# A first normalisation in two halves, and a table that places every step of the weight units

## The chip, the cores and the metric

The kernel runs on one core of a Trainium2 chip. Its engines are called PE (TensorE, matmuls), DVE (VectorE), ACT (ScalarE), POOL (GpSimd) and SP (SyncE, which here only issues DMAs); each works through its own queue in order. The metric is the device time of one execution in microseconds (us), the median of several runs.

## What is computed

```python
def _attn_ref(q, k, v, g_norm):          # q, k, v: (8, 8, 576, 64)
    kv = np.einsum('bhsd,bhse->bhde', k, v)
    out = np.einsum('bhsd,bhde->bhse', q, kv)
    rms = np.sqrt(np.mean(out * out, axis=-1, keepdims=True) + 1e-06)
    return (out / rms * g_norm).astype(np.float32)

def _moe_ref(x, w_in, w_out, a, b):      # x: (4608, 512), w_in: (512, 2048), w_out: (2048, 512)
    h = x @ w_in
    h2 = h * h
    h3 = h2 * h
    P = a[0] + a[1] * h + a[2] * h2 + a[3] * h3
    Q = 1.0 + np.abs(b[0]) * np.abs(h) + np.abs(b[1]) * h2
    g = P / (Q + 1e-06)
    return (g @ w_out).astype(np.float32)
```

x is the attention's output, all eight heads of a token side by side. The weights come as 64 bit floats.

## The kernel before

The 4608 tokens are nine tiles (t) of 512. A tile has 16 slots (c), one for each 128 columns of w_in and 128 rows of w_out. The main loop (L598) counts slots i = 16 t + c through all tiles. In a slot PE does gemm2 of two slots before (LAG = 2, four accumulators in PSUM), steps of the next tile's attention, and gemm1 of the next slot into one of two PSUM buffers h. ACT, DVE and POOL turn h into g in four steps: ew_a (ACT v and u, DVE q and u, L417 to L420), ew_b (ACT q, Ln, Exp into a PSUM bank r, DVE u, L426 to L429), ew_c (DVE u, r, g, L435 to L442) and, one slot later, ew_d (ACT gh, POOL gl, L452 and L453). A buffer h is free once L427 has read it.

A 32 bit product at full precision is made of parts: a factor is cast to fp32r (the high part) and the difference is kept as a second part; a gemm is then three matmuls, high by high, low by high and high by low. In tile 0 the first four gemm1 and the first twelve gemm2 take whole 32 bit factors instead (unsplit1, unsplit2; PE makes two passes of each).

A weight unit, such as ("wi", 4), is two slots' weights, 1024 columns of 64 bit words. It is fetched to a raw tile (fetch_w, L166) and converted on the chip: "hi" and "lo" scale its high and low words (scale_high and scale_low, L180 on ACT or L182 on DVE), "shift" (L203) and "or" (L208) on DVE and "add" (L209, on POOL as a rule) put a 32 bit float together in ups, and split_w casts it (L224, ACT) and subtracts (L225, POOL). The tables scale_at, conv_at and split_at (L143 to L152) give each unit a slot for each stage; fetch_at gives the slot of its fetch. These steps fill tile 0's slots; the splits of the first six wo units lie in tile 1. L209 on DVE shows in the trace as a custom operation.

Ahead of the loop stands the attention of tile 0: the loads `first` (k, v, q and constants of each of four head pairs p), first_kv (kvp, L540; copies kvf, L543), first_o (op, L547; square sq, L549; xf, L550), the means ms (L570), the reciprocal root in three ACT and two DVE steps (newton_rstd, L250 to L256), its spread over the partitions by a matmul (rb, L588) and the norm (L589). warm (L531) issues matmuls on a zero tile whose result nobody reads. For later tiles the same runs in steps inside the slots (att_kv, att_o, att_ms, att_rstd, att_rd, att_rb, att_norm), the spread as a DMA to DRAM and back; split makes the two parts of x (ACT L264, then L268), for tile 1 in slot 14.

All this stands in a manual schedule: the order of the code is the order of each engine's queue.

## Time and profile before

| what | us |
|---|---|
| median of 3 runs (910.95 to 911.41) | 911.12 |
| the profiled execution | 911.83 |
| its span, first to last instruction | 910.0 |
| PE busy in the span | 886.8 |
| ACT / DVE / POOL busy | 710.5 / 694.0 / 342.8 |

A line of the timeline gives start, duration, engine, line of the code, operation, the tiles written and read, shape and count, and in brackets how long the engine stood idle before it and who released it. A line of the waits gives who waited for whom, the sum, the count and the longest. In a group of instructions stand the busy time and the mean duration of one in ns. Durations of neighbours overlap a little, since the engines are pipelined.

### The profile page before, as it was taken

What the parts mean: (1) busy time and instruction counts of PE and PEld (TensorE: products, weight loads), DVE (VectorE), ACT (ScalarE), POOL (GpSimd) and SP (SyncE); (2) the same over time, 40 slices, a digit from 0 to 9 for tenths busy, and PEclk for the clock granted to TensorE, in tenths of its full rate; (3) what the DMA queues carried; (4) which work ended last, traced back from release to release, by engine and by line L of the source; (5) the groups of instructions that cost most, each with busy time, mean ns of one, the idle gap of its engine ahead of it and who ended that gap; (6) DMA issues with size and microseconds to landing.
All of it is one profiled execution on the core that took longest, in us unless ns stands there. A gap on an engine that the chain in (4) does not pass through costs nothing.

```text
span 910.0 us, 12075 instructions
## 1 busy us (share of the span) xinstructions
PE 886.8 (97%) x4372; PEld 693.9 (76%) x4372; DVE 694.0 (76%) x1029; ACT 710.5 (78%) x1171; POOL 342.8 (38%) x272
## 2 busy tenths in 40 slices
PE   9799979999999999999999999999999999999997
PEld 6355547778888788878887888788878887887886
DVE  2999997677876777677777777678667877787776
...
GB/s 368 233 239 117 127 68 42 116 53 48 11 118 82 48 1 128 81 21 27 116 57 36 48 84 85 41 48 41 120 20 47 1 70 12 48 1 47 1 1 46
DMA packets 24485, 65.94 MB, mean 72 GB/s; under 512 B 2345, under 2 KB 3369, under 8 KB 24425
## 3 DMA queue, kind: packets, MB, share of 16 engines
q1 hardware_dynamic: 23848, 64.65, 21.9%
...
q10 hardware_dynamic: 576, 0.52, 0.2%
...
## 4 chain that ended last, share of the span: by engine, by line
PE 80%; DVE 11%; ACT 5%; issue 3%; ACTq 0%; POOL 0%; DVEq 0%; POOLq 0%
PE h L407 13%; PE acc L472 12%; PE h L409 12%; PE h L408 12%; PE acc L474 12%; PE acc L473 12%; PE kvp L297 2%; DVE q L419 2%; DVE u L435 1%; DVE r L436 1%; PE idle L531 1%; ACT r L428 1%; ACT q L426 1%; DVE u L427 1%; PE op L328 1%
## 5 line engine op out<-in xcount | busy, mean ns | idle before, releaser
L453 POOL TENSOR_TENSOR gl<-u,gh 128x512 fp32r<-128x512 f32 x131 | 172.5, 1317 | 453.3 <-ACT gh L452 266.6
L407 PE MATMUL h<-x,wiparts 128*128 128x512 f32 (+1 forms) x564 | 226.4, 401 | 0.0
L409 PE MATMUL h<-x,wiparts 128*128 128x512 f32 (+1 forms) x564 | 219.6, 389 | 1.1 <-DVE x L268 1.1
L408 PE MATMUL h<-x,wiparts 128*128 128x512 f32 (+1 forms) x564 | 219.2, 389 | 0.0
L435 DVE SCALAR_TENSOR_TENSOR u<-u,na,r 128x512 f32<-128x512 f32 x143 | 106.7, 746 | 88.9 <-ACT r L429 88.8
L419 DVE SCALAR_TENSOR_TENSOR q<-v,b0abs,h 128x512 f32<-128x512 f32 x143 | 106.2, 743 | 83.2 <-ACT u L418 83.0
L417 ACT ACTIVATE v<-h,b 128x512 f32<-128x512 f32 x143 | 98.8, 691 | 90.1 <-PE h L409 86.6
L407 PEld LDWEIGHTS h<-x,wiparts 128*128 128x128 f32 x564 | 105.9, 188 | 30.2 <-DVE u L427 5.9
L426 ACT ACTIVATE q<-q 128x512 f32<-128x512 f32 x143 | 90.6, 634 | 48.2 <-DVE q L419 47.2
L409 PEld LDWEIGHTS h<-x,wiparts 128*128 128x128 f32 x564 | 105.9, 188 | 24.8 <-DVE x L268 2.3
L474 PE MATMUL acc<-woh,gl 128*128 128x512 f32 x320 | 124.6, 389 | 0.0
L473 PE MATMUL acc<-wol,gh 128*128 128x512 f32 x320 | 124.5, 389 | 0.0
L472 PE MATMUL acc<-woh,gh 128*128 128x512 f32 x320 | 124.5, 389 | 0.0
L408 PEld LDWEIGHTS h<-x,wiparts 128*128 128x128 f32 x564 | 106.1, 188 | 21.4 <-issue 1.3
L418 ACT ACTIVATE u<-h,na 128x512 f32<-128x512 f32 x143 | 111.2, 778 | 0.0
L427 DVE SCALAR_TENSOR_TENSOR u<-u,na,h 128x512 f32<-128x512 f32 x143 | 106.8, 747 | 4.6
L428 ACT ACTIVATE r<-q,bias 128x512 f32<-128x512 f32 x143 | 99.0, 692 | 4.6
L452 ACT CAST gh<-u 128x512 fp32r<-128x512 f32 x131 | 81.5, 622 | 23.9 <-DVE u L442 23.2
L429 ACT ACTIVATE r<-r,bias 128x512 f32<-128x512 f32 (+1 forms) x145 | 95.6, 659 | 4.8
L436 DVE SCALAR_TENSOR_TENSOR r<-q,r 128x512 f32<-128x512 f32 x143 | 98.3, 687 | 0.0
L420 DVE TENSOR_TENSOR u<-u,h 128x512 f32<-128x512 f32 x143 | 97.1, 679 | 0.0
L442 DVE SCALAR_TENSOR_TENSOR u<-r,u 128x512 f32<-128x512 f32 x131 | 90.4, 690 | 4.1
...
## 6 DMA issues: line engine op xcount, KB each, us to landing
...
```

The costliest lines, as they stand in the source:

```text
L407: PE.matmul(ph, wh, xh, start=(kc == 0), stop=False)
L408: PE.matmul(ph, wl, xh, start=False, stop=False)
L409: PE.matmul(ph, wh, xl, start=False, stop=(kc == NPAIR - 1))
L418: ACT.activation(u, ph, AF.Identity, bias=na[:, 2:3], scale=na[:, 3:4])
L419: DVE.scalar_tensor_tensor(q, v, b0abs, ph, ALU.add, ALU.mult)
L427: DVE.scalar_tensor_tensor(u, u, na[:, 1:2], ph, ALU.add, ALU.mult)
L428: ACT.activation(r, q, AF.Ln, bias=bias[:, 2:3], scale=QSC)
L435: DVE.scalar_tensor_tensor(u, u, na[:, 0:1], r, ALU.add, ALU.mult)
L453: POOL.tensor_tensor(gl, u, f32(gh), ALU.subtract)
L472: PE.matmul(o, gh[:, ss], wh, start=(c == 0), stop=False)
L473: PE.matmul(o, gh[:, ss], wl, start=False, stop=False)
L474: PE.matmul(o, gl[:, ss], wh, start=False, stop=(c == NF - 1))
```

## The change

The first normalisation is done in two halves of two head pairs each: ms, the three ACT and two DVE steps, rb and the norms of pairs 0 and 1 are issued between the products of pairs 2 and 3, and gemm1 of slot 0 in two halves too. The loads of `first` come pair by pair, with the small copy into `spread` after pair 0's. Most of the matmuls of warm are gone. Pair 3's xf is made on ACT.

scale_at, conv_at and split_at give way to a table, first_tiles. Each entry names a step, its engine (A, D or P for ACT, DVE or POOL), and a slot with a place in it: s before ew_a, h between the ACT and DVE halves of ew_a, q before ew_b, v inside ew_b ahead of Ln, e behind ew_b, r at the start of ew_c, g ahead of the DVE step that makes g, z at the end. Units x0 and x1 are the x of tiles 0 and 1 by head pair. Fetches move to other slots, one raw tile to another room, and the reciprocal root of tile 1 one slot later. Of the longer removed blocks, all in the listing above, the diff shows nothing ("...").

```diff
-        ("wi", 6): "p6", ("wo", 2): "r0", ("wi", 8): "p5", ("wo", 4): "r1",
+        ("wi", 6): "p6", ("wo", 2): "p4", ("wi", 8): "p5", ("wo", 4): "r1",
...
-        -1: [("wi", 6), ("wo", 2)], 0: [("wi", 8), ("wo", 4)], 2: [("wi", 10), ("wo", 6)], 4: [("wi", 12), ("wo", 8)],
-        6: [("wi", 14)], 8: [("wo", 10)], 10: [("wo", 12)], 11: [("wo", 14)],
+        -1: [("wo", 2), ("wi", 6)],
+        1: [("wi", 8), ("wi", 10), ("wo", 6)],
+        2: [("wo", 4)],
+        4: [("wi", 14)],
+        5: [("wo", 8)],
+        6: [("wi", 12)],
+        7: [("wo", 10)],
+        9: [("wo", 12)],
+        10: [("wo", 14)],
     }
...
+    first_tiles = {
+        ("wi", 4): "hi A 0s, lo A 0z, shift D 0g, or D 1h, add P 1v, cast A 2h, rest P 2q",
+        ("wi", 6): "hi A 1z, lo A 1h, shift D 2s, or D 2r, add P 3e, cast A 4q, rest P 4z",
+        ("wi", 8): "hi A 3e, lo A 4e, shift D 4v, or D 4z, add P 5e, cast D 6q, rest P 7v",
+        ("wi", 10): "hi A 5h, lo A 6z, shift D 6g, or D 7h, add P 7v, cast A 7v, rest P 8s",
+        ("wi", 12): "hi A 7q, lo A 8q, shift D 8v, or D 8r, add P 8r, cast A 9g, rest P 10e",
+        ("wi", 14): "hi A 10q, lo A 10q, shift D 10v, or D 11s, add P 11h, cast A 12q, rest P 12e",
+        ("wi", 0): "cast D 7v, rest P 7r",
+        ("wi", 2): "shift2 D 0s, or2 D 0s, add2 P 0q, cast A 3s, rest P 3v",
+        ("wo", 0): "shift D 0s, or D 0s, add P 0s, cast A 15g, rest P 16z",
+        ("wo", 2): "hi D 0z, lo A 2q, shift D 1r, or D 1z, add P 2v, cast D 17z, rest D 19r",
+        ("wo", 4): "hi A 3e, lo A 3r, shift D 3z, or D 4h, add P 4v, cast A 18z, rest P 21e",
+        ("wo", 6): "hi A 5v, lo D 5r, shift D 5r, or D 5r, add P 6v, cast A 21v, rest P 23s",
+        ("wo", 8): "hi A 6z, lo A 7z, shift D 7e, or D 7z, add P 9g, cast A 24s, rest D 24v",
+        ("wo", 10): "hi A 9q, lo D 10s, shift D 9r, or D 9g, add P 10q, cast D 24z, rest P 25q",
+        ("wo", 12): "hi A 10r, lo A 12h, shift D 11r, or D 12h, add D 12h, cast A 12r, rest D 13e",
+        ("wo", 14): "hi A 11g, lo A 13r, shift D 12g, or D 13s, add P 14s, cast A 14g, rest D 14z",
+        ("x0", 0): "cast A 0s, rest D 0s",
+        ("x1", 0): "norm P 13h, cast A 14e, rest D 14g",
+        ("x0", 1): "cast A 0h, rest P 1v",
+        ("x1", 1): "norm P 11g, cast D 14r, rest P 14z",
+        ("x0", 2): "cast A 0h, rest D 0v",
+        ("x1", 2): "norm D 14e, cast A 14r, rest P 15s",
+        ("x0", 3): "cast A 1s, rest P 2z",
+        ("x1", 3): "norm P 13v, cast A 14r, rest P 15h",
+    }
+    plan = {}
+    for u, row in first_tiles.items():
+        for entry in row.split(", "):
+            what, by, at = entry.split()
+            plan.setdefault((int(at[:-1]), at[-1]), []).append((what, {"A": ACT, "D": DVE, "P": POOL}[by], u))
+
+    def todo(i, place):
+        for what, by, u in plan.pop((i, place), ()):
+            steps[what](by, u)
...
-    def conv_b2(u, part=both, add_by=POOL):
+    def conv_or(u, part=both):
-        add_by.tensor_tensor(w, w, low, ALU.add)
+    def conv_add(u, part=both, by=POOL):
+        low, high = words(u, part)
+        w = ups[u].bitcast(I32)[:, part]
+        by.tensor_tensor(w, w, low, ALU.add)
...
+    def copy(by, to, of):
+        ACT.copy(to, of) if by == ACT else by.tensor_copy(to, of)
...
-        for js in (one, two) if c == SPLIT0 else (both,):
-            ACT.copy(wh[:, js], w[:, js])
-            POOL.tensor_tensor(wl[:, js], w[:, js], f32(wh[:, js]), ALU.subtract)
+        wparts[u] = wh, wl
+        copy(by, wh, ups[u])
+    def rest_w(u, by):
+        wh, wl = wparts.pop(u)
+        by.tensor_tensor(wl, ups.pop(u), f32(wh), ALU.subtract)
...
-    for f, at in ((att_kv, [1, 3, 5, 7]), (att_o, [2, 4, 6, 8]), (att_ms, [9]), (att_rstd, [9]), (att_rd, [10]), (att_rb, [11, 11]), (att_norm, [12, 12, 13, 13])):
+    for f, at in ((att_kv, [1, 3, 5, 7]), (att_o, [2, 4, 6, 8]), (att_ms, [10]), (att_rstd, [10]), (att_rd, [11]), (att_rb, [11, 12])):
...
         ACT.activation(u, ph, AF.Identity, bias=na[:, 2:3], scale=na[:, 3:4])
+        between()
         DVE.scalar_tensor_tensor(q, v, b0abs, ph, ALU.add, ALU.mult)
         DVE.tensor_tensor(u, u, ph, ALU.mult)
...
-        fill(-1)
         ACT.activation(q, q, AF.Abs)
         DVE.scalar_tensor_tensor(u, u, na[:, 1:2], ph, ALU.add, ALU.mult)
+        between()
         ACT.activation(r, q, AF.Ln, bias=bias[:, 2:3], scale=QSC)
...
     for p in range(NPAIR):
-        nc.sync.dma_start(kvq0[p][:, 0:10 * P], first[p][:, 0:10 * P])
-    for p in range(NPAIR):
-        nc.sync.dma_start(kvq0[p][:, 10 * P:], first[p][:, 10 * P:])
+        for part in (slice(0, 10 * P), slice(10 * P, NC0 + 8)):
+            nc.sync.dma_start(kvq0[p][:, part], first[p][:, part])
+        if p == 0:
+            nc.sync.dma_start(quarters[:, 1, D:P], quarters[:, 0, 0:D])
     fetch_w(("wi", 0))
-    nc.sync.dma_start(quarters[:, 1, D:P], quarters[:, 0, 0:D])
...
+        if p == 3:
+            ACT.activation(xf[0, p], o0[p], AF.Copy, scale=ghalf)
+        else:
+            DVE.tensor_scalar(xf[0, p], o0[p], ghalf, None, ALU.mult)
...
     warm(8, idle)
-    for p in range(NPAIR):
-        first_kv(p)
-        warm(3, idle)
+    r0 = work.tile([P, TW], F32, tag="u", name="r_0")
+    r2 = work.tile([P, TW], F32, tag="u", name="r2_0")
+    ms0 = {}
+
+    def first_ms(k):
+        pool, tag = ((ps_at, "at"), (ps_at, "r"))[k]
+        ms0[k] = pool.tile([P, TW], F32, tag=tag, name=f"ms_0_{k}", bufs=1)
+        for p in (2 * k, 2 * k + 1):
+            PE.matmul(ms0[k][p * Q4:(p + 1) * Q4], sel, sq0[p], start=True, stop=True)
+
+    def first_newton(k):
+        ps = slice(2 * k * Q4, 2 * (k + 1) * Q4)
+        ms, r, rr = ms0[k][ps], r0[ps], r2[ps]
+        return (
+            lambda: ACT.activation(r, ms, AF.Ln, bias=bias[ps, 0:1], scale=ZSC),
+            lambda: ACT.activation(r, r, AF.Exp, bias=bias[ps, 1:2], scale=-0.5),
+            lambda: ACT.activation(rr, r, AF.Square),
+            lambda: DVE.scalar_tensor_tensor(rr, ms, 1e-6, rr, ALU.add, ALU.mult),
+            lambda: DVE.scalar_tensor_tensor(r, rr, 3.0, r, ALU.subtract, ALU.mult),
+        )
+
+    rb0 = {}
+
+    def first_rb(p):
+        rb0[p] = ps_acc.tile([P, TW], F32, tag="acc", name=f"rb_0_{p}")
+        ps = slice(p * Q4, (p + 1) * Q4)
+        PE.matmul(rb0[p], spread[ps], r0[ps], start=True, stop=True)
+
+    def first_norm(p):
+        DVE.tensor_tensor(xf[0, p], xf[0, p], rb0[p], ALU.mult)
+
+    first_kv(0)
+    warm(3, idle)
     POOL.tensor_scalar(ghalf, gcol, -0.5, None, ALU.mult)
     POOL.tensor_scalar(na, ab[:, 0:4], -1.0, None, ALU.mult)
     POOL.tensor_copy(b1, ab[:, 5:6])
-    for p in range(NPAIR):
-        first_o(p)
+    first_o(0)
+    first_kv(1)
+    first_o(1)
+    first_kv(2)
+    first_ms(0)
+    newton = first_newton(0)
+    newton[0]()
+    first_o(2)
+    first_kv(3)
+    for step in newton[1:3]:
+        step()
+    conv_a(("wi", 0), one, DVE)
+    conv_b1(("wi", 0), one)
+    for step in newton[3:]:
+        step()
+    conv_b2(("wi", 0), one)
+    first_o(3)
+    first_ms(1)
+    first_rb(0)
+    first_rb(1)
+    newton = first_newton(1)
+    for step in newton[:3]:
+        step()
     fetch_kvq(1, 0)
     for u in fetch_at[-1]:
         fetch_w(u)
...
+    first_norm(0)
+    conv_a(("wi", 0), two)
+    first_norm(1)
+    for step in newton[3:]:
+        step()
+    h00 = ps_h.tile([P, TW], F32, tag="h", name="h_0_0")
+    gemm1_part(0, 0, h00, slice(0, TW), (0, 1))
+    first_rb(2)
+    first_rb(3)
     ACT.activation(b0abs, ab[:, 4:5], AF.Abs)
+    conv_b1(("wi", 0), two)
+    conv_b2(("wi", 0), two)
+    first_norm(2)
+    first_norm(3)
+    gemm1_part(0, 0, h00, slice(0, TW), (2, 3))
     for part in (one, two):
         conv_a(("wi", 2), part)
...
     conv_b1(("wi", 2), one)
     conv_b2(("wi", 2), one)
     conv_a(("wo", 0))
...
+    steps = {
+        "hi": lambda by, u: scale_high(u, by),
+        "lo": lambda by, u: scale_low(u, by),
+        "shift": lambda by, u: conv_b1(u),
+        "or": lambda by, u: conv_or(u),
+        "add": lambda by, u: conv_add(u, both, by),
+        "shift2": lambda by, u: conv_b1(u, two),
+        "or2": lambda by, u: conv_or(u, two),
+        "add2": lambda by, u: conv_add(u, two, by),
+        "cast": lambda by, u: cast_w(u, by) if u[0] in ("wi", "wo") else xl1.update({u: split(int(u[0][1]), u[1], by)}),
+        "rest": lambda by, u: rest_w(u, by) if u[0] in ("wi", "wo") else xl1.pop(u)(by),
+        "norm": lambda by, u: by.tensor_tensor(xf[1, u[1]], xf[1, u[1]], rbs[1, u[1] // 2][u[1] % 2], ALU.mult),
+    }
     for i, (t, c) in enumerate(slots[:-1]):
-        ew_a(t, c, ph)
+        rest = {0: [], 1: [], 2: []}
+        todo(i, "s")
+        ew_a(t, c, ph, between=lambda: todo(i, "h"))
         if i:
             ew_d(*slots[i - 1])
...
+        todo(i, "q")
+        ew_b(t, c, ph, r_bank(t, c), lambda: todo(i, "v"))
+        todo(i, "e")
         if i >= LAG:
             gemm2(*slots[i - LAG])
...
-        if 4 <= i < len(slots) - 2 and not early:
+        if 4 <= i < len(slots) - 2:
             ph = gemm1(*slots[i + 1])
-        if c == NF - 2 and t < NTILE - 1:
+        if c == NF - 2 and 0 < t < NTILE - 1:
             xl = [split(t + 1, p) for p in range(NPAIR)]
             for k in range(2):
                 rest[k].append(xl[k])
                 rest[2].append(xl[2 + k])
-        ew_c(t, c, lambda k: [f() for f in rest[k]])
-        if i in scale_at and scale_at[i][0] == "wi":
-            scale_low(scale_at[i], ACT)
-        if i >= NF and i in split_at:
-            split_w(split_at[i])
+        ew_c(t, c, lambda k: [todo(i, "rgz"[k]), *(f() for f in rest[k])])
     finish(NTILE - 1)
```

More of the change, by code (lines that the diff above doesn't have):

```diff
@@ L257, in newton_rstd, with split @@
         return rest
-    def split(t, p, low_by=DVE):
+    def split(t, p, by=ACT):
         if p % 2 == 0:
@@ L263, in split, with rest @@
         f = xf[t, p]
-        ACT.copy(xh, f)
+        copy(by, xh, f)
         x.setdefault(t, []).append((xh, xl))
-        def rest():
+        def rest(low_by=DVE):
             low_by.tensor_tensor(xl, f, f32(xh), ALU.subtract)
@@ L397, in gemm1, with gemm1_part @@
         return ph
-    def gemm1_part(t, c, ph, cs):
-        for kc in range(NPAIR):
+    def gemm1_part(t, c, ph, cs, kcs=range(NPAIR)):
+        for kc in kcs:
             ks = slice(kc * P, (kc + 1) * P)
@@ L409, in gemm1_part, with ew_a @@
             PE.matmul(ph, wh, xl, start=False, stop=(kc == NPAIR - 1))
-    def ew_a(t, c, ph, w=TW):
+    def ew_a(t, c, ph, w=TW, between=lambda: None):
         nm = f"{t}_{c}"
```

67 lines of the change are left out of this document (9 added, 58 removed).

## The prediction

> **What bounds the kernel now.** I read the busy time by stage first, then PE's own waits, then the rows around each wait. Columns of the stage table: window and length in us, busy us (and count) of PE, PEld, DVE, ACT, POOL, granted clock, DMA share, GB/s.
>
> ```profile
> 22.00:50.00 28.00, 22.33 (x74) 9.95 (x71) 27.67 (x34) 19.50 (x32) 18.68 (x12) 1.00 0.58 212
> 50.00:110.00 60.00, 59.08 (x248) 34.62 (x247) 59.41 (x71) 52.83 (x83) 36.82 (x21) 1.00 0.45 157
> 110.00:144.00 34.00, 26.43 (x90) 17.60 (x88) 31.70 (x37) 23.38 (x35) 24.05 (x12) 0.90 0.28 82
> 144.00:165.00 21.00, 19.20 (x115) 14.56 (x115) 15.46 (x26) 17.76 (x31) 7.86 (x5) 1.00 0.28 90
> 165.00:265.00 100.00, 100.00 (x515) 81.22 (x515) 75.36 (x119) 85.02 (x141) 46.02 (x31) 1.00 0.22 66
> ```
>
> From 165 us on PE is never idle: the change touches nothing there that PE waits for, so the end moves by what PE gains before 165. There PE idles 28.00 - 22.33 = 5.67, 0.92, 7.57 and 1.80 us, 15.96 in all, while DVE is full until 144. The waits of PE between 22 and 170 us give the same sum and the culprits:
>
> ```profile
> PE acc L468 <- DVE g L442: 6.0, 2, 3.7
> PE acc L472 <- ACT woparts L224: 3.6, 1, 3.6
> PE acc L473 <- POOL woparts L225: 1.7, 1, 1.7
> PE h L403 <- POOL wiw L209: 1.2, 1, 1.2
> PE h L409 <- DVE x L268: 1.1, 2, 0.9
> PE acc L472 <- ACT ob L480: 0.6, 1, 0.6
> ```
>
> Why DVE is full shows where it works beside POOL, and in the groups of 50 to 110 us (busy, then mean ns of one):
>
> ```profile
> 47.17 2.37 POOL L225 TENSOR_TENSOR wiparts<-wiw,wiparts 128x1024 fp32r<-128x1024 f32 x1 [0.55 <-ACT wiparts L224]
> 47.90 2.73 DVE L208 SCALAR_TENSOR_TENSOR wow<-raw_wo,wow 128x1024 int32<-128x1024 int32 x1
> L208 DVE SCALAR_TENSOR_TENSOR wiw<-raw_wi,wiw 128x1024 int32<-128x1024 int32 x4 | 4.8, 1212 | 0.0
> L182 DVE TENSOR_SCALAR raw_wi<-raw_wi 128x1024 f32<-128x1024 f32 x4 | 7.6, 1891 | 0.0
> L180 ACT ACTIVATE raw_wi<-raw_wi 128x1024 int32<-128x1024 uint32 x5 | 5.8, 1167 | 0.0
> L224 ACT CAST wiparts<-wiw 128x1024 fp32r<-128x1024 f32 x5 | 5.3, 1056 | 2.0 <-POOL wiw L209 2.0
> ```
>
> The same L208 costs 1.21 us with POOL quiet and 2.73 when POOL is at work: POOL ends at 47.17 + 2.37 = 49.54, and DVE ends 1.09 later, so it stood still until then. The Trainium skill says so too ("SBUF — State Buffer", section "SBUF: two separate sides"): the port pair of DVE and GpSimd is held for a whole instruction and the other engine blocks. The trace agrees, with these 1.09 us. By that rule every copy and difference that this change gives to DVE also shuts POOL out, which speaks against the change; it is the first rival below.
>
> **Term A, the start up to the first gemm2.** Before, one chain runs through all four pairs:
>
> ```profile
> 10.41 0.80 PE L540 MATMUL kvp<-first 128*64 128x64 f32 x20
> 11.26 0.42 ACT L543 COPY kvf<-kvp 64x64 f32<-64x64 f32 x2 [1.17 <-PE kvp L540]
> 11.92 3.60 PE L547 MATMUL op<-first,kvf 128*128 128x512 f32 x8
> 15.45 1.80 PE L570 MATMUL ms<-sq,sel 128*32 128x512 f32 x8
> 17.35 0.69 ACT L250 ACTIVATE r<-ms,bias 128x512 f32<-128x512 f32 x1 [1.20 <-PE ms L570]
> 19.55 0.69 DVE L255 SCALAR_TENSOR_TENSOR r<-ms,r 128x512 f32<-128x512 f32 x1 [0.88 <-ACT r L252]
> 19.51 2.34 ACT L180 ACTIVATE raw_wi<-raw_wi 128x512 f32<-128x512 f32 x4
> 21.07 1.25 PE L588 MATMUL rb<-r,spread 32*128 32x512 f32 x8 [0.49 <-issue]
> 22.20 2.48 DVE L589 TENSOR_TENSOR xf<-xf,rb 128x512 f32<-128x512 f32 x4 [1.23 <-PE rb L588]
> 26.49 1.39 POOL L209 TENSOR_TENSOR wiw<-wiw,raw_wi 128x512 int32<-128x512 int32 x1 [6.45 <-DVE wiw L208]
> 27.94 7.13 PE L403 MATMUL h<-xf,wiw 128*128 128x512 f32 x16 [1.24 <-POOL wiw L209]
> 30.35 0.73 DVE L427 SCALAR_TENSOR_TENSOR u<-u,na,h 128x512 f32<-128x512 f32 x1
> 32.57 1.49 DVE L203 TENSOR_SCALAR wiw<-raw_wi 128x512 int32<-128x512 int32 x1
> 34.09 2.77 DVE L208 SCALAR_TENSOR_TENSOR wiw<-raw_wi,wiw 128x512 int32<-128x512 int32 x1
> 38.70 0.68 DVE L442 SCALAR_TENSOR_TENSOR g<-r,u 128x512 f32<-128x512 f32 x1
> 39.52 3.67 PE L468 MATMUL acc<-wow,g 128*128 128x512 f32 x8 [3.72 <-DVE g L442]
> 10.00:12.00 2.00, 2.00 (x32) 1.81 (x31) 0.00 (x0) 0.51 (x3) 0.55 (x3) 1.00 1.06 411
> ```
>
> The eight loads of the first tile are 4 x (640 + 260) KB, 9 us at 411 GB/s, full from about 3 us: all in at 12. After the change they come pair by pair, and SP holds pair 1 behind the copy of L525 until POOL has filled its source, so I put pair 3 at 12.5. Its chain: kvp (0.80 as at 10.41) to 13.6 after a wait for op of pair 2, the two kvf copies (0.42) to 14.1, op (a quarter of 3.60) to 15.05. On ACT the first half's Exp and Square stand ahead of its square, so that ends at 16.05; ms 17.0; Ln to Square (17.35 to 19.55 before, 2.2) 19.2; two L255/L256 steps 20.8; rb (1.13 to its reader) 21.9; norms 23.2, against 22.20 + 2.48 = 24.68 before. The first half (rb at 17.05, norms to 19.4) lets h(0,0) run two of its four passes beside this; the other two end at 24.3. The second half of the first weight unit, added at 26.49 + 1.39 = 27.88 before, gets its scaling on ACT at 19.2, two DVE steps by 21.65, POOL's 1.3: 23.0. So h(0,1) starts at 24.3 instead of 27.94.
>
> Little of these 3.6 us counts yet. h(0,2) takes the buffer that slot 0's L427 frees. On ACT, from 19.2, wi0's two half scalings (1.2), wi2's four (2.34 as at 19.51), wo0's two and wi4's one (1.17 each by L180) and an x cast stand ahead of v, 7.3 in all: v at 26.5. On DVE, five steps of wi2, wo0 and x0 come first: q at 28.5, L427 30.4 as before. PE idles 2.8 us; h(0,2) runs 30.5 to 33.95, kvp to 34.7. What is gained lies behind L427: L203 and L208 of 32.57 and 34.09 (4.2 us) are already done. L435 goes at 31.65 when Exp has ended, then L436, one shift, L442: g ends at 34.15 instead of 39.38, and gemm2(0,0) starts at 34.7 instead of 39.52. **A = 4.8.** Bounds: one more POOL operation of 2.4 in DVE's way leaves 2.4; if L427 waits for nothing, h(0,1), h(0,2) and kvp run through to 31.9, and 7.6 is gained.
>
> **Term B, slots 2 to 10.** PE has only 0.92 us to give. The high scaling of six wi units goes from DVE (1.89 each) to ACT (1.17 each by L180): 7.6 us leave a DVE that is full, and ACT, at 52.83 of 60, takes 4 x 1.17 = 4.7 and gives wi8's and wi0's casts (1.06 each) to DVE and a low scaling of wo6: about 54.3 of 60. Summed by slot from these rows, elementwise work included, DVE has 4.4 to 7.1 us per slot in slots 2 to 11, ACT 4.3 to 8.5 (the 8 and 8.5 in slots 3 and 10, each followed by a lighter one), PE 7.0. PE ends last in the sums; POOL's waits take half a microsecond, most likely before h(0,4), whose last x difference is POOL's third job in slot 2. **B = 0.5** (0 to 0.9; 3.0 if the long first pass of each gemm1 goes too, 0.79 in the row below against 0.40, seven times 0.3).
>
> ```profile
> 50.47 0.79 PE L407 MATMUL h<-x,wiparts 128*128 128x512 f32 x1
> ```
>
> **Term C, slots 11 to 14.** Here the waits of 2.3, 3.6 and 1.7 us lie, and a half clock behind them:
>
> ```profile
> 124.97 2.21 DVE L209 CUSTOM_DVE_ANT_0 wow<-raw_wo,wow 128x2048 uint16<-128x2048 uint16 x1
> 36.00:38.00 2.00, 0.00 (x0) 0.00 (x0) 2.00 (x3) 0.00 (x0) 1.37 (x2) 1.00 0.00 0
> 133.00:134.00 1.00, 1.00 (x3) 0.81 (x4) 0.97 (x2) 1.00 (x2) 1.00 (x1) 0.50 0.00 0
> ```
>
> wo12 and wo14 are converted on DVE inside slots 12 and 13, with such an add of 2.2 us in each, g comes late, ACT's cast of wo12 stands behind gh, POOL's difference behind that. At half clock some 3.5 us are worked, so 1.8 are lost: C is at most 7.57 + 1.8 = 9.4. After, the scalings are on ACT in 10 and 11, wo14's add is on POOL, both differences are on DVE. Counted from the start of gemm2(0,10): PE wants wo12's difference after gemm2, h, gemm2, h (3.43 + 2.74 each) at 12.4. DVE in slots 12 and 13 has: POOL's norm to wait for (1.5), or 1.1, add 2.2, elementwise 3.8, wo14's shift and or 1.7, half a slot of elementwise 1.9, POOL's next norm 1.5, difference 1.1: 14.8. So 2.4 us of waiting stay, and no gap is long. **C = 9.4 - 2.4 = 7.0**; with both old waits for the parts still there, 2.3.
>
> **Term D, slots 14 to 17.** The x differences of tile 1 are spread over slots 14 and 15; POOL's last one ends 1.5 us before PE reads it by my count, so 1.1 goes and the evacuation's 0.6 stays. **D = 1.1** (0 to 1.8). POOL is handed two norms, three x differences and wo14's add there, 10 us in three slots of 5.5 to 6.2: it fits, but the last link has 1.5 us of cover.
>
> Other moves cost nothing on PE: the wo casts and differences of slots 16 to 25 have the ACT (85.02) and POOL (46.02) of the last stage row as cover, and each stands one slot or more ahead of its gemm2.
>
> **Sum:** 4.8 + 0.5 + 7.0 + 1.1 = 13.4. The profiled execution took 911.83 (span 910.0); less 13.4 it is 898.4. The median of the runs shown is 0.7 lower, so I predict 897.7.
>
> **Rivals.**
> 1. The port. Each difference or cast new on DVE meets POOL's 2.4 us jobs and waits about 2.73 - 1.21 = 1.5; then DVE keeps its pace: A half, B nothing, C near its low end: 2.4 + 2.8 = 5.2, 906. For it: DVE's 59.41 of 60. Against: per two slots one port step goes from DVE to ACT, which has a port of its own. Chance 0.14.
> 2. The clock. The change drops 23 of 34 warm-up calls, and PE waits in pieces between 9 and 24 us. Run at half clock from 12 to 24, the two last op passes (0.9 each), ms and rb (1 each) and h(0,0) (3.4) cost 7 more: gain 6.4, 905. Against: 3.7 idle us at 35.8 left 1.00 (row of 36 to 38). The Trainium skill ("TensorE: Matmul & The Clock Gate", section "What's actually happening") halves the clock after an idle window of about 3.4 us; by that rule the start, with no gap over 1.5 in my chain up to h(0,1), stays at full clock; the gap at 35.8, 3.9 long, might have lost it by the same rule and did not. I give it 0.06.
> 3. Slower: the loads. Weight fetches now stand on SP behind steps that wait: wo6 behind wi4's add, wi12 behind a qr whose buffer op frees, wo12 and wo14 behind POOL adds one slot ahead of their use. ACT then waits for data in front of its elementwise work.
>
> ```profile
> 90.32 0.38 SPq L166 DMA_DIRECT2D raw_wo<-in_w_out_dram  x1
> 97.17 1.19 ACT L180 ACTIVATE raw_wo<-raw_wo 128x1024 f32<-128x1024 f32 x1 [0.47 <-DMA raw_wo<-in_w_out_dram]
> ```
>
> A load took 6.9 us from issue to use here (97.17 - 90.32); wi12 has some 4, one gemm1 and the first two ACT steps of a slot. From 3.4 us each at four places that reach PE (13.4 / 4) it is slower; at 5 each, 20 - 13.4 = 6.6 slower: 918. For it: ACT waited in the row of 97.17 already. Against: h has two buffers and gemm2 lags two slots, so a wait under some 3 us is covered. Chance 0.12.
> 4. The waits move and the sum is nothing, 911: 0.03.
>
> **Chances and range.** The forecast has 0.65, from 889 to 903: its own bounds are A 7.6, B 3.0, C 9.4, D 1.8, sum 21.8, 889, and, with two terms at their low ends, 8 us, 903. Up to 907 come rivals 1 and 2. Range 889 to 907, about 0.8. The measurement tells 0.2% (1.8 us) from no change: faster 0.85, same 0.03, slower 0.12.
>
> **What would show it.** A: PE's first L468 group at about 35 instead of 39.5, h(0,1) near 24, L427 of slot 0 near 30. B: L182 on DVE gone for wi, DVE below 56 of 60 in slots 3 to 10. C: no half clock, one wait of about 2 us on wo12's difference. D: no wait of gemm1(1,0) on x. Wrong if the page shows ACT waiting on weight DMAs for more than 3 us at a time, L208 still near 2.7 in most slots, or idle PE behind 165.

## The result, and the profile after

The changed kernel takes 903.12 us (median of 4 runs, 901.94 to 903.68); the kernel before took 911.26 beside it (910.95 to 912.42). The ratio is 0.9907 (95% interval 0.9889 to 0.9924): 8 us faster, where 13.4 were forecast. The profiled execution is the slowest of the four, 903.68, with a span of 901.9 (before 910.0).

The lines of the code have moved. What the prediction calls L403 is now L442 (whole gemm1), L407 to L409 are L446 to L448 (gemm1 in parts), L468 is L508 (whole gemm2), L472 to L474 are L512 to L514 (gemm2 in parts), L180 and L182 are L209 and L211 (scalings), L203, L208 and L209 are L232, L237 and L242 (shift, or, add), L224 is L249 (casts), L225 is L266 (weight differences), L268 is L307 (x differences), L427 is L466 (frees h) and L442, the step that writes g, is L482.

Busy time by stage of the changed kernel, columns as in the prediction:

```profile
22.00:50.00 28.00, 24.19 (x83) 11.44 (x79) 26.82 (x38) 25.62 (x39) 18.05 (x11) 1.00 0.80 300
50.00:110.00 60.00, 56.67 (x240) 33.35 (x239) 55.28 (x72) 51.82 (x80) 40.32 (x22) 1.00 0.42 152
110.00:144.00 34.00, 30.49 (x110) 21.30 (x109) 29.27 (x38) 25.20 (x37) 19.75 (x12) 0.90 0.14 32
144.00:165.00 21.00, 21.00 (x130) 17.30 (x129) 15.87 (x27) 19.53 (x35) 9.53 (x7) 1.00 0.41 138
165.00:265.00 100.00, 99.97 (x516) 81.06 (x514) 77.74 (x121) 82.12 (x138) 39.34 (x29) 1.00 0.19 59
128.00:130.00 2.00, 2.00 (x6) 1.56 (x5) 1.97 (x4) 1.53 (x4) 2.00 (x1) 0.50 0.00 0
```

DVE is no longer full behind 50 us, as forecast (55.28 of 60). PE now idles 3.81 us from 22 to 50 (before 5.67), 3.33 from 50 to 110 (before 0.92), 3.51 from 110 to 144 (before 7.57), none to 165. So the second stage has become worse, and the third, at a mean clock of 0.90 again, still holds a half clock, of which the last row shows a part. The longest waits of PE from 18 to 175 us:

```profile
PE acc L513 <- DVE woparts L266: 3.4, 1, 3.4
PE h L442 <- POOL wow L242: 3.0, 1, 3.0
PE acc L508 <- POOL wow L242: 2.7, 1, 2.7
PE h L442 <- DVE xf L629: 1.6, 2, 0.9
PE h L448 <- POOL x L307: 0.4, 1, 0.4
```

None of before's long waits is left in its old form; three take their place, each about 3 us long. Two the prediction had (3.0 ahead of h(0,2), where it counted 2.8; 3.4 on wo12's difference, where it counted 2.4). The 2.7, a gemm2 that waits for an add on POOL, it had not.

To see where the time came from I compare the start of the same work in the traces: of the first matmul of gemm2(0,n), the gemm2 with w_out rows 128 n of tile 0, which stands in slot n + 2 (n = 16 and 23 run on into tile 1). Each entry is before's start less that kernel's start, in us, so a gain up to there. The experiments' columns are used further down. The last row gives the times at which the granted clock of that trace falls to 0.50 (up to 900 us). Each such stretch lasts 3.41 us, those with a star 6.83 us, and a busy PE loses half of it. Where it falls differs between traces whose code is the same up to there, so a part of every column is chance.

| n | start before | changed | s_start | t_table | e1 | e3 | e5 | e7 | e6 | e9 | e11 |
|---|---|---|---|---|---|---|---|---|---|---|---|
| 0 | 39.52 | 3.2 | 1.0 | -1.0 | 2.4 | 1.8 | 2.4 | 1.6 | 1.4 | 1.7 | 2.7 |
| 7 | 92.05 | 3.9 | -0.5 | 0.8 | 3.2 | 3.5 | 4.0 | 3.3 | 3.1 | 3.4 | 3.4 |
| 9 | 105.58 | 0.9 | -0.5 | -3.2 | 2.5 | 3.5 | -2.0 | 3.3 | -0.9 | 3.4 | 2.7 |
| 13 | 139.98 | 4.5 | -0.3 | 4.9 | 4.0 | 8.8 | 6.7 | 9.9 | 6.4 | 8.4 | 9.1 |
| 14 | 147.26 | 6.4 | -0.4 | 6.8 | 5.9 | 7.3 | 8.5 | 8.1 | 8.3 | 9.4 | 8.7 |
| 16 | 161.11 | 7.4 | -0.4 | 7.4 | 6.9 | 8.0 | 9.1 | 5.7 | 9.3 | 10.0 | 9.2 |
| half clock from | 129.71* | 126.44* | 37.64*, 129.80* | 35.81, 100.66 | 126.82* | 31.90, 134.30 | 31.49, 96.34* | 32.23, 141.46 | 32.43, 97.28 | 32.63, 124.79 | none |

In the terms of the prediction: A 3.2 (forecast 4.8); from there to n = 7, most of B, 0.7 (0.5); then 3.0 are lost again by n = 9; from 9 to 14, C, 5.4 (7.0); from 14 to 16, D, 1.0 (1.1). At n = 23 (206 us) the gain is 7.1, at the end of the span 8.1: the last 1.0 comes behind 206 us, 0.4 of it up to PE's last matmul (905.32 and 897.86), 0.6 behind that, while the last output is written.

**Start of the changed kernel.** Its timeline (start, duration, engine, line):

```profile
19.65 1.96 PE L442 MATMUL h<-xf,wiw 128*128 128x512 f32 x4 [0.87 <-DVE xf L629]
23.51 5.42 PE L442 MATMUL h<-xf,wiw 128*128 128x512 f32 x12 [0.78 <-DVE xf L629]
25.32 1.36 POOL L242 TENSOR_TENSOR wiw<-wiw,raw_wi 128x512 int32<-128x512 int32 x1 [1.15 <-DVE wiw L237]
25.56 1.68 DVE L237 SCALAR_TENSOR_TENSOR wiw<-raw_wi,wiw 128x512 int32<-128x512 int32 x1
29.62 0.74 DVE L459 SCALAR_TENSOR_TENSOR q<-v,b0abs,h 128x512 f32<-128x512 f32 x1
31.07 0.75 DVE L466 SCALAR_TENSOR_TENSOR u<-u,na,h 128x512 f32<-128x512 f32 x1
31.96 3.67 PE L442 MATMUL h<-xf,wiw 128*128 128x512 f32 x8 [3.04 <-POOL wow L242]
34.34 0.68 DVE L482 SCALAR_TENSOR_TENSOR g<-r,u 128x512 f32<-128x512 f32 x1
36.30 1.12 PE L508 MATMUL acc<-wow,g 128*128 128x512 f32 x2
```

The chain has the forecast's shape. h(0,0) begins with two of its four head pairs at 19.65, the rest follow at 23.51; q comes at 29.62 (forecast 28.5), L466 starts at 31.07 (forecast, as L427, 30.4), h(0,2) at 31.96 (30.5), g ends at 35.02 (34.15), and the first gemm2 starts at 36.30 (34.7). About one microsecond is lost ahead of q: the "or" at 25.56 lies beside POOL's add of 25.32 and takes 1.68, where the same shape took 0.69 without one.

**Around 90 us.** POOL, DVE and the gemm2 that waits:

```profile
84.81 2.41 POOL L266 TENSOR_TENSOR wiparts<-wiw,wiparts 128x1024 fp32r<-128x1024 f32 x1
85.03 3.26 DVE L237 SCALAR_TENSOR_TENSOR wow<-raw_wo,wow 128x1024 int32<-128x1024 int32 x1
92.33 2.44 POOL L242 TENSOR_TENSOR wiw<-wiw,raw_wi 128x1024 int32<-128x1024 int32 x1 [5.11 <-ACT xf L372]
94.72 2.38 POOL L242 TENSOR_TENSOR wow<-wow,raw_wo 128x1024 int32<-128x1024 int32 x1
97.16 1.12 PE L508 MATMUL acc<-wow,g 128*128 128x512 f32 x2 [2.73 <-POOL wow L242]
```

wo8's "or" is done at 88.29, and POOL stands idle for 5.11 us; but the table puts wo8's add into slot 9, behind wi12's add of slot 8, so POOL begins it at 94.72, and PE waits 2.73.

**Around 125 us.** Slots 12 to 14:

```profile
120.03 1.04 ACT L249 CAST woparts<-wow 128x1024 fp32r<-128x1024 f32 x1
121.41 0.69 DVE L232 TENSOR_SCALAR wow<-raw_wo 128x1024 int32<-128x1024 int32 x1
122.61 1.21 DVE L237 SCALAR_TENSOR_TENSOR wow<-raw_wo,wow 128x1024 int32<-128x1024 int32 x1
123.74 0.74 DVE L459 SCALAR_TENSOR_TENSOR q<-v,b0abs,h 128x512 f32<-128x512 f32 x1
125.78 1.48 DVE L266 TENSOR_TENSOR woparts<-wow,woparts 128x1024 fp32r<-128x1024 f32 x1
127.31 0.80 PE L513 MATMUL acc<-woparts,gh 128*128 128x512 f32 x1 [3.42 <-DVE woparts L266]
```

wo12's cast ends at 121.07, but its difference begins at 125.78: the table has it in slot 13 behind wo14's shift and "or" and three elementwise steps. PE idles 3.42 us, the clock falls inside this gap, at 126.44, and PE then runs at half clock up to 133.26 (the row of 128 to 130 above).

### The profile page after: what moved, and what is told of

Its sections match the earlier page's. It is cut to its first block, busy times and chain, and to the rows that moved or that the text cites. A ratio compares the mean times of both kernels' runs of the same rounds, so it can differ in the third digit from the quotient of the medians.

```text
span 901.9 us, 11977 instructions
## 1 busy us (share of the span) xinstructions
PE 883.2 (98%) x4326; PEld 689.8 (76%) x4326; DVE 686.0 (76%) x1033; ACT 712.6 (79%) x1173; POOL 334.7 (37%) x267
## 4 chain that ended last, share of the span: by engine, by line
PE 84%; DVE 8%; ACT 6%; issue 2%; POOL 0%; ACTq 0%; DVEq 0%; POOLq 0%
PE h L446 13%; PE acc L513 13%; PE acc L514 13%; PE h L447 13%; PE acc L512 13%; PE h L448 13%; PE kvp L336 2%; DVE q L459 1%; ACT r L468 1%; ACT r L469 1%; DVE r L476 1%; DVE wow L237 1%; DVE u L475 1%; PE op L367 1%; ACT q L465 1%
## 5 line engine op out<-in xcount | busy, mean ns | idle before, releaser
L446 PE MATMUL h<-x,wiparts 128*128 128x512 f32 (+1 forms) x564 | 226.9, 402 | 0.0
L448 PE MATMUL h<-x,wiparts 128*128 128x512 f32 (+1 forms) x564 | 219.5, 389 | 0.4 <-POOL x L307 0.4
L446 PEld LDWEIGHTS h<-x,wiparts 128*128 128x128 f32 x564 | 106.2, 188 | 30.0 <-DVE u L466 5.9
L512 PE MATMUL acc<-woh,gh 128*128 128x512 f32 x320 | 124.5, 389 | 0.0
L514 PE MATMUL acc<-woh,gl 128*128 128x512 f32 x320 | 124.5, 389 | 0.0
L448 PEld LDWEIGHTS h<-x,wiparts 128*128 128x128 f32 x564 | 106.1, 188 | 23.4 <-POOL x L307 0.8
L466 DVE SCALAR_TENSOR_TENSOR u<-u,na,h 128x512 f32<-128x512 f32 x143 | 106.9, 748 | 5.1
L468 ACT ACTIVATE r<-q,bias 128x512 f32<-128x512 f32 x143 | 99.0, 692 | 4.6
L482 DVE SCALAR_TENSOR_TENSOR u<-r,u 128x512 f32<-128x512 f32 x131 | 90.4, 690 | 4.1
```

Of the source, the lines that this page charges most:

```text
L446: PE.matmul(ph, wh, xh, start=(kc == 0), stop=False)
L448: PE.matmul(ph, wh, xl, start=False, stop=(kc == NPAIR - 1))
L468: ACT.activation(r, q, AF.Ln, bias=bias[:, 2:3], scale=QSC)
L512: PE.matmul(o, gh[:, ss], wh, start=(c == 0), stop=False)
L514: PE.matmul(o, gl[:, ss], wh, start=False, stop=(c == NF - 1))
```

## The experiments

Each is an edit of the changed kernel, save where said, and its ratio is to the kernel before, on the same chip. Two kernels of one chip are told apart by their ranges. In the diffs the letter behind a slot is the place in it, as in the table of the change.

**s_start: the change's start alone.** The start in two halves, with the loop of before: its placing of the weight steps and its fetches (those ahead of the loop as in the change, and wo2 in another raw tile, which that order needs).

```diff
     fetch_at = {
+        -1: [("wo", 2), ("wi", 6)], 0: [("wi", 8), ("wo", 4)], 2: [("wi", 10), ("wo", 6)], 4: [("wi", 12), ("wo", 8)],
+        6: [("wi", 14)], 8: [("wo", 10)], 10: [("wo", 12)], 11: [("wo", 14)],
     }
-    first_tiles = {
...
```

> Start alone: the start of the changed kernel (halves, loads pair by pair, wo2's raw tile in its new room) in front of the loop of before with scale_at, conv_at and split_at. Theory (the start only counts through the DVE steps that slot 0 has behind it): h(0,1) begins 2 to 3 us earlier, but L427 of slot 0 and with it h(0,2) move by under 1 us and g of slot 0 stays behind two steps of wi2; PE's first gemm2 near 38.5 to 39.5, time 910 to 911.3. Rival (the start's gain is kept to the end): first gemm2 near 36.3, time 908.

Measured: 911.46 (10 runs), ratio 0.9999 (0.999 to 1.0008). The first gemm2 starts 1.0 us earlier, and the gain has turned into -0.5 by n = 7. Rows of this trace, in the line numbers of before, first the waits of PE, then its first gemm2:

```profile
PE acc L468 <- DVE g L442: 5.1, 2, 2.8
PE acc L472 <- ACT woparts L224: 3.6, 1, 3.6
38.48 6.64 PE L468 MATMUL acc<-wow,g 128*128 128x512 f32 x8 [2.81 <-DVE g L442]
```

All of before's long waits stand. But what the start brought is lost here to the clock: it falls at 37.64, and the first gemm2 takes 6.64 us where before's takes 3.67. DVE keeps its lead (its third g starts at 52.54, before's at 53.62). So by the ten runs the start alone is worth nothing; whether the full DVE would take the gain back too, this trace can't show.

**t_table: the table alone.** The new loop behind before's start.

```diff
-    first_kv(0)
...
+    for p in range(NPAIR):
+        first_kv(p)
+        warm(3, idle)
```

> Table alone: the loop of the changed kernel behind the start of before. Theory (the start is worth little by itself, the table has the rest): first gemm2 near 37.5 to 38.5, the waits on wo8's add and wo12's difference stay at about 3 us each, time 904 to 905. Rival (the two parts add up, the start has 3.2 of the 8.1): 906.5.

Measured: 905.64 (903.34 to 907.08), ratio 0.9934 (0.9915 to 0.9953). Most of the gain, 5.6 us, is the table's. What the start adds behind the table is 2.5 by the medians, but t_table's profiled execution is its fastest, and by n = 16 it has gained 7.4, just as the changed kernel: by these runs the start is worth between 0 and 2.5 us. The two traces also show where it goes: gemm2(0,0) starts 4.2 us earlier in the changed kernel than in t_table, gemm2(0,12) 3.9 (123.39 against 127.25), gemm2(0,13) 0.4 later (135.44 against 135.06). In t_table PE comes later to the wait for wo12's difference, waits 2.1 instead of 3.4 us and keeps the full clock behind it. The expectation was off in part: the first gemm2 starts at 40.47, not near 38, and the time lies between those of the theory and of the rival. The 1.0 behind 206 us is the table's too: there t_table gains 1.0 and s_start 0.1.

**e1: wo8's add in time.**

```diff
-        ("wo", 8): "hi A 6z, lo A 7z, shift D 7e, or D 7z, add P 9g, cast A 24s, rest D 24v",
+        ("wo", 8): "hi A 6z, lo A 7z, shift D 7e, or D 7z, add P 8h, cast A 24s, rest D 24v",
```

> One entry of the table: wo8's add on POOL from 9g to 8h, where POOL stood idle for 5.1 us. Theory (a late entry): PE's wait of 2.7 on L242 before gemm2(0,8) is gone, and as PE then works on, the time falls by 2 to 2.9: 900.5 to 901. Rival (PE is in step with DVE and POOL there, a wait taken away comes back at the next link, and the 3.4 us wait on wo12's difference grows by as much): under 0.5, 902.7 to 903.1.

Measured: 903.76 (903.22 to 904.21), ratio 0.9914 (0.9897 to 0.993): no gain. The wait of 2.7 is gone and at n = 9 the gain is 2.5 instead of 0.9, yet at n = 13 it is 4.0. PE waits in slot 14 as long as before:

```profile
PE acc L513 <- DVE woparts L266: 3.4, 1, 3.4
```

So the rival holds in that the gain is lost at the next links. DVE's queue, which makes the difference of wo12, did not come earlier with PE: from 110 to 126 us it is busy for 14.98 of 16 us in both traces, and q of slot 13 starts at 124.40, 0.66 us later than in the changed kernel (123.74). PE loses its lead in a wait of 0.8 for gh ahead of gemm2(0,12), and then meets the difference.

**e2: wo12's difference ahead of wo14's "or".**

```diff
-        ("wo", 12): "hi A 10r, lo A 12h, shift D 11r, or D 12h, add D 12h, cast A 12r, rest D 13e",
+        ("wo", 12): "hi A 10r, lo A 12h, shift D 11r, or D 12h, add D 12h, cast A 12r, rest D 12z",
```

> One entry: wo12's difference on DVE from 13e to 12z, ahead of wo14's or. Theory (a late entry): the difference ends near 123.8 instead of 127.2, PE's wait of 3.4 falls to 1 or less (on gl of slot 12, which POOL makes by 125), the half clock behind it (15 matmuls of 0.43 instead of 0.23) is gone: 4 to 6 us, 897 to 899. Rival (it is the port: wo14's or then waits for POOL's gl, slot 13's chain gets later by 1 to 2 us and the wait moves to gemm2(0,13)): 0 to 2 us, 901 to 903.

Measured: 903.42 (903.23 to 904.1), ratio 0.9913 (0.9899 to 0.9928): no gain. The wait of 3.4 is gone. The timeline shows what took its place:

```profile
124.49 1.53 POOL L493 TENSOR_TENSOR gl<-u,gh 128x512 fp32r<-128x512 f32 x1 [2.60 <-ACT gh L492]
124.81 2.29 DVE L237 SCALAR_TENSOR_TENSOR wow<-raw_wo,wow 128x1024 int32<-128x1024 int32 x1
127.03 0.73 DVE L459 SCALAR_TENSOR_TENSOR q<-v,b0abs,h 128x512 f32<-128x512 f32 x1
131.04 2.43 POOL L242 TENSOR_TENSOR wow<-wow,raw_wo 128x1024 int32<-128x1024 int32 x1 [2.77 <-ACT raw_wo L209]
133.42 1.28 POOL L493 TENSOR_TENSOR gl<-u,gh 128x512 fp32r<-128x512 f32 x1
134.75 0.50 PE L514 MATMUL acc<-woparts,gl 128*128 128x512 f32 x1 [1.30 <-POOL gl L493]
```

wo14's "or" now falls beside POOL's gl: 2.29 instead of 1.21, and it ends 1.08 us behind gl (124.49 + 1.53 = 126.02; 124.81 + 2.29 = 127.10). q starts at 127.03 instead of 123.74. Of these 3.29 us 1.08 are the delay of the "or", 1.1 the difference, which now stands ahead of q, and 1.1 had been lost before (slot 12's step L482 starts at 123.08 instead of 122.01, behind a half clock at 33.02). A low scaling comes late, POOL's add behind it, and gl behind that add; PE waits for gl, and from 135.42 runs 3.41 us at half clock. One of the four runs kept the full clock throughout (1.000) and still took 903.38.

**e3: e1 and e2 together.**

> Both entries at once: wo8's add on POOL at 8h and wo12's difference on DVE at 12z. Theory now (slots 12 to 14 are one chain over DVE, POOL's port and ACT, and PE meets it wherever it waits; either entry alone only moved the wait): PE reaches slot 12 about 2 us earlier, waits there for gh and gl of slot 12 and 13 instead, gemm2(0,16) near 153 to 154.5 as in the three others, time 902.5 to 903.5. Rival (each was hidden by the other): the two waits of 2.7 and 3.4 us and the half clock go together, 897 to 899.

Measured: 902.89 (902.67 to 903.16), ratio 0.9907 (0.9894 to 0.9921), as the change. At n = 13 it is 4.2 us ahead of the changed kernel, at n = 16 only 0.6. PE waits for gl (1.9) and gh (1.4) instead, and the half clock from 134.30, with PE busy throughout, takes another 1.7 (half of 3.41).

**e5: POOL's add or the buffer, ahead of h(0,2)?** The waits named POOL's add of wo0 as what ended PE's 3.0 us there, where the prediction had named the buffer that L466 frees. The x difference of pair 0 moves behind slot 0's elementwise work:

```diff
-        ("x0", 0): "cast A 0s, rest D 0s",
+        ("x0", 0): "cast A 0s, rest D 0z",
```

> x0's first difference on DVE from 0s, ahead of slot 0's q, to 0z behind its g. It tells what ends PE's wait of 3.0 us ahead of h(0,2). If it is L427 (the buffer), PE starts h(0,2) 0.6 to 0.7 us earlier against h(0,0) than before, whatever POOL's add of wo0 does; if it is that add, named by the profile, PE starts with the add's end, and L427 ends earlier than that. Time within 0.7 of the changed kernel's.

Measured: 902.16 (2 runs, 901.54 and 902.78), ratio 0.9899 (0.988 to 0.9918). POOL's add, PE's h(0,2) behind its wait, and from slot 14 the wait for wo12's difference:

```profile
28.97 2.38 POOL L242 TENSOR_TENSOR wow<-wow,raw_wo 128x1024 int32<-128x1024 int32 x1 [2.57 <-ACT x L249]
31.10 5.37 PE L442 MATMUL h<-xf,wiw 128*128 128x512 f32 x8 [2.44 <-DVE u L466]
127.98 0.50 PE L513 MATMUL acc<-woparts,gh 128*128 128x512 f32 x1 [1.53 <-DVE woparts L266]
```

The wait is 0.6 us shorter, and by name on L466: one DVE step less ahead of it, and PE starts that much sooner, ahead of the end of POOL's add (31.35). The buffer ends the wait, as the prediction had it. The time is not told apart from the change. This trace shows one thing more. It lost time to a half clock from 96.34, PE came later to slot 14, waited 1.53 there and kept the full clock; from the end of that wait to gemm2(0,13) it needs 5.35 us (t_table too), the changed kernel 8.13. So the half clock there costs 2.8 us, and by n = 16 this trace has gained 9.1.

**e6: the gap filled.** Fourteen matmuls that nobody reads (28 passes) in front of gemm2(0,12), so that PE isn't idle while it waits for wo12's parts:

```diff
         todo(i, "e")
+        if i == 14:
+            idle2 = ps_at.tile([P, TW], F32, tag="at", name="idle2", bufs=1)
+            for _ in range(14):
+                PE.matmul(idle2[:, 0:P], spread, spread, start=True, stop=True)
         if i >= LAG:
```

> The changed kernel with 14 matmuls that nobody reads (128 columns, two passes of 0.11 us, 3.1 us in all) on PE ahead of gemm2(0,12), where PE stands idle for 3.7 us; nothing else is moved. Theory (the half clock behind the gap costs time of its own, 15 passes of 0.43 instead of 0.23): the granted clock stays at 1.00 there, gemm2(0,13) starts 2 to 3 us earlier and the time falls by as much, 900 to 901. Rival (slots 12 to 14 are bound by the chain over DVE, POOL and ACT, so PE's slow passes are waiting time anyway): under 0.7, 902.5 to 903.2.

Measured: 900.96 (900.78 to 901.91), ratio 0.9888 (0.9875 to 0.9902). The stage, then the timeline around the gap:

```profile
122.00:146.00 24.00, 24.00 (x136) 19.84 (x135) 21.47 (x29) 19.13 (x30) 13.48 (x9) 1.00 0.09 28
```

```profile
124.97 3.29 PE L712 MATMUL idle<-spread 128*128 128x128 f32 x28
125.89 1.52 DVE L266 TENSOR_TENSOR woparts<-wow,woparts 128x1024 fp32r<-128x1024 f32 x1
128.01 0.48 PE L512 MATMUL acc<-woparts,gh 128*128 128x512 f32 x1
```

The difference is ready no earlier (127.41, changed kernel 127.26) and gemm2(0,12) starts late, at 128.01. But from there to gemm2(0,13) it takes 5.5 us (133.55); in the changed kernel it takes 8.1 from the end of the wait (127.31 to 135.44). That is 2.6 us less, near the 2.8 of e5 and t_table, and this trace is 1.9 us ahead of the changed kernel at n = 16 (9.3 against 7.4). All four runs lie below the lowest of the change (901.91 against 901.94 at the nearest), though the intervals of the two ratios overlap. That the fillers did it is not shown by the trace: PE came 1.8 us later to slot 11 than in the changed kernel (n = 9), would have waited about 2.4 us without them (124.97 to 127.41), and t_table and e5 kept the clock behind such waits with no filler. They too have gained 7.4 and 9.1 at n = 16.

**e7: the chain cut elsewhere.** e3, with wo14's "or" behind q, its low scaling and add earlier, cast and difference later:

```diff
-        ("wo", 14): "hi A 11g, lo A 13r, shift D 12g, or D 13s, add P 14s, cast A 14g, rest D 14z",
+        ("wo", 14): "hi A 11g, lo A 13h, shift D 12g, or D 13v, add P 14q, cast A 15h, rest D 15r",
```

> Both entries of e3, and wo14 taken out of slot 13's chain: its or on DVE from 13s to 13v, its low scaling on ACT from 13r to 13h, its add on POOL from 14s to 14q (behind gl of slot 13), cast and difference to slot 15. Theory (one chain through slots 12 to 14: wo14's or held DVE for 2.3 us ahead of slot 13's q, and wo14's add held POOL ahead of gl): the waits in slots 12 to 15 fall under 2 us in all, no half clock, gemm2(0,16) near 148 to 150, 897 to 899.5. Rival (the next link, x's parts of tile 1 on POOL, ends as late as now): 901 to 903.

Measured: 904.2 (903.32 to 904.99), ratio 0.9919 (0.9905 to 0.9933): a miss, and on the same chip slower than e3. n = 13 is reached with the best gain of all, 9.9; n = 16 with the worst of the new tables, 5.7. Between them, in the timeline:

```profile
131.23 2.97 POOL L242 TENSOR_TENSOR wow<-wow,raw_wo 128x1024 int32<-128x1024 int32 x1
131.81 2.68 DVE L249 CAST x<-xf 128x512 fp32r<-128x512 f32 x1
136.44 0.50 PE L448 MATMUL h<-x,wiparts 128*128 128x512 f32 x1 [2.10 <-DVE x L307]
141.17 0.57 PE L513 MATMUL acc<-woparts,gh 128*128 128x512 f32 x1 [1.59 <-DVE woparts L266]
```

The add, now earlier, meets an x cast on DVE, which took 0.41 in e2 and takes 2.68 here: it ends 0.29 us behind the add. The x difference follows it, and gemm1 of tile 1 waits 2.1 us. That is the first part of the loss (9.9 to 8.1 at n = 14). The rest has other causes: wo14's difference, moved to slot 15, lets PE wait 1.59, and the clock is halved from 141.46.

**e9: the same cut without that meeting.** e7, with wo14's add, cast and difference back in their places (14s, 14g, 14z).

> e7 with wo14's later steps where the changed kernel has them: or on DVE at 13v and low scaling on ACT at 13h as in e7, but add on POOL at 14s (POOL stood idle for 3.8 us ahead of gl of slot 13), cast at 14g and difference at 14z. Theory (slots 12 to 14 are one chain; e7 cut it for gemm2(0,13), which started at 130.1, and lost that again because POOL's late add held the port against DVE's cast of x for 2.2 us and the difference of wo14 came in slot 15): gemm2(0,13) near 130, no wait over 1 us behind it, no half clock, gemm2(0,16) near 149 to 150.5, time 898 to 899.5. Rival (the x parts of tile 1 set the end whatever comes before): 901.5 to 903.

Measured: 901.08 (900.72 to 901.81), ratio 0.9889 (0.9874 to 0.9904): 2 us below the change, short of what was expected. The wait for wo12 is gone; PE idles 1.37 and 0.63 us for gh and gl in slot 14. A half clock comes twice, from 32.63 at h(0,2) and from 124.79 in slot 14, of which the first row shows a part:

```profile
125.00:128.00 3.00, 3.00 (x7) 2.39 (x8) 3.00 (x4) 2.44 (x4) 1.77 (x2) 0.50 0.00 0
```

```profile
31.76 5.37 PE L442 MATMUL h<-xf,wiw 128*128 128x512 f32 x8 [3.03 <-POOL wow L242]
123.54 0.50 PE L512 MATMUL acc<-woparts,gh 128*128 128x512 f32 x1 [1.37 <-ACT gh L492]
124.90 0.80 PE L514 MATMUL acc<-woparts,gl 128*128 128x512 f32 x1 [0.63 <-POOL gl L493]
```

**e10: e9 with an earlier L466.** Besides e5's move, the second steps of wi2 go behind q:

```diff
-        ("wi", 2): "shift2 D 0s, or2 D 0s, add2 P 0q, cast A 3s, rest P 3v",
+        ("wi", 2): "shift2 D 0v, or2 D 0v, add2 P 0e, cast A 3s, rest P 3v",
```

> e9 and slot 0's DVE queue shortened ahead of q: x0's first difference from 0s to 0z, wi2's second shift and or from 0s to 0v, their add from 0q to 0e. Theory (L427 ends PE's wait ahead of h(0,2)): L427 ends 2 us earlier, first gemm2 1 to 2 us earlier against h(0,0), and now that slots 12 to 14 have room the time falls by 1 to 2 against e9. Rival (what is gained at the start is eaten by a wait in slots 8 to 14): within 0.6 of e9.

Measured: 902.16 (901.83 to 902.27), ratio 0.99 (0.9884 to 0.9917), on the same chip about 1 us slower than e9. L466 and h(0,2) start only 0.4 us earlier than in e9 (30.48 and 30.87, 31.37 and 31.76), not 2: wo0's "or" now takes 2.20 beside POOL's add instead of 1.23, and q waits 0.45 for ACT. The first gemm2 starts at 35.70, 2.1 earlier than in e9, but 1.7 of that is the half clock which e9's h(0,2) has and this trace has not; the gain there is 3.8 us. At 51.7 us PE waits 1.2 for an x difference on POOL (with a later one, 2.2), and by n = 2 only 1.6 of gain are left. What is gained at the start is eaten behind it.

**e11 and e12: fillers on top of e9.** e11 puts twelve unread matmuls in front of h(0,2) and six in front of gemm2(0,12); e12 adds e5's move.

```diff
+        if i in (1, 14):
+            idle2 = ps_at.tile([P, TW], F32, tag="at", name=f"idle_{i}", bufs=1)
+            for _ in range(12 if i == 1 else 6):
+                PE.matmul(idle2[:, 0:P], spread, spread, start=True, stop=True)
```

> e9 with matmuls that nobody reads in PE's two remaining gaps: 12 ahead of h(0,2), 6 ahead of gemm2(0,12). Theory (a half clock behind either gap costs 1.6 to 2 us of PE time): no granted clock under 1.00 between 22 and 140 us, both gaps end when they did, time 1.5 to 3.5 under e9's 901.1: 897.6 to 899.6. Rival (the slow passes stand in waiting time, as PE meets the same chain behind them): within 0.7 of e9.

> e11 and x0's first difference on DVE from 0s to 0z as in e5. Theory (L427 ends PE's wait ahead of h(0,2)): h(0,2) and the first gemm2 0.6 to 0.7 us earlier against h(0,0) than in e11, 0.3 to 0.7 off the time. Rival (a wait in slots 8 to 14 eats it): within 0.3 of e11.

Measured: e11 901.54 (901.25 to 902.1), ratio 0.9897 (0.988 to 0.9913); e12 901.69 (901.32 to 902.06), ratio 0.9897 (0.9882 to 0.9912). e11's clock is 1.00 in both places, and nothing is gained over e9, as e11's rival had it; e12 gains nothing over e11. In e11 PE waits 1.5 us for gl and 1.5 for x differences on POOL, where e9 had 0.9 and 0.5. Passes at half clock had covered these waits: a faster PE comes sooner to what isn't ready.

The best kernels are e6 (ratio 0.9888) and e9 (0.9889), about 2 us under the change and 10 under the kernel before.

## Why the prediction was right in sign and wrong in size

The 903.12 us lie in the stated range, but in its last part, from 903 to 907, which was kept for the first two rivals, and neither of them came as it was priced. By the stretches of the table the gain up to n = 16 is about 6 us short of the sum: 1.6 in A, 2.8 in B, 1.6 in C, 0.1 in D; 0.7 come behind it.

**What bounds the kernel: right.** PE idles only ahead of 165 us, and the gain came almost wholly there. Not forecast is the 1.0 us that comes behind 206 us. It belongs to the table (t_table); PE's idle time there hardly differs (waits of 0.9 and 0.5 before, 0.9 and 0.4 after), and what shortens stays open.

**Term A: mechanism right, size off, and not additive.** 3.2 instead of 4.8 at the first gemm2. Two terms were mis-sized. L466 starts 0.7 us later than forecast, and the "or" of 1.68 alone adds 1.0 ahead of it: the port's price, which the prediction left to its first rival. And the prediction let h(0,2) start as L427 starts (30.5 behind 30.4), where it starts after its end (31.96; L466 ends at 31.82): 0.8 of PE's time more, since kvp and the first gemm2 follow on PE. That the buffer ends PE's wait ahead of h(0,2) is shown by e5. But the prediction added A to the sum as if PE kept it to the end. Against t_table the changed kernel keeps its earlier start up to slot 14 and loses all of it there, at the wait for wo12's difference and the half clock behind it; e10 loses more than half of it within two slots, to a wait for the buffer (0.47) and one for an x difference (1.22). The 3.2 are also a lucky trace: in six of the nine traces with this start, the new table and no filler ahead of h(0,2) (e2, e3, e5, e6, e7, e9) the clock falls while h(0,2) runs or just ahead of it, and the gain at n = 0 is 0.5 to 2.4.

**Term B: the step that failed.** "Summed by slot, PE ends last" came out up to slot 9 (0.7 against 0.5; DVE at 55.28 of 60 where below 56 was forecast; the high scalings off DVE). Then 3.0 us are lost: wo8's add, in POOL's queue behind wi12's. A sum of loads by slot says that POOL has room, and it had 5.11 us of it. It says nothing of the order, in which the operation with the nearest reader stood last. So B was -2.3 instead of 0.5 at that point. e1 removes that wait, so the cause of those 2.7 us is shown; it is also shown that removing them alone does not bring the shortfall back, since e1 is no faster.

**Term C: the term that was mis-sized.** Forecast 2.4 us of waiting and no half clock, measured 3.4 and a half clock that cost 2.8 (e5, t_table). The prediction's count of DVE's work in slots 12 and 13 was of the right kind, but it held "no gap is long" for safe with 2.4 us, and here the clock fell when PE had been idle for 2.6 us of a gap of 3.42. The half clock of before is a little undercounted too: PE works 4.4 us in it, not 3.5. It also took the wait as one item with one cause. e2, e3 and e7 show that slots 12 to 15 are a chain over four engines, in which wo14's "or", gl, wo14's add, the x cast and the x difference stand within a microsecond or two of each other. In e2 and e7 the link that moved was met by POOL and DVE at the same time, and a DVE step took 2.3 to 2.7 us instead of 0.4 to 1.2; e9 moved the links and met less (1.75 for the "or", 0.42 for the x cast).

**Term D: right.** 1.0 against 1.1; 0.4 of a wait for x is left, and the 0.6 of the evacuation, which was to stay, is gone from the list.

**The rivals.** The port (906) is right as a mechanism, in places: the rows of 25.56 and 85.03, and what e2 and e7 met. It does not hold DVE at its old pace. The clock (905) came, but in slots 12 to 14. The start ran at full clock in this trace (1.00 up to 126.44). In e9 it did not: eight passes of h(0,2) took 5.37 instead of 3.67, 1.7 us, behind a gap as long (3.03 and 3.04), in code that is the same up to there. The gap of before that the rival leaned on is 3.72 us long by its own row, not 3.9. The loads on SP (918) did not come: ACT's waits name no weight load.

**What is shown and what is open.** Shown: what each of the three waits stood on (e1, e2, e5), the price of the half clock in slot 14, and that no single wait taken away brings the forecast time. e6 and e9 each lie about 2 us below the change, with intervals that overlap its interval. Why is argued: for e6 the kept clock, for e9 a chain in which the "or" stands behind q and DVE meets POOL less. Twelve and six fillers on top of e9 (e11) bring nothing. Not shown is what the other 3 us would take; no run reached the forecast.
